# An attention and SwiGLU kernel rewritten: 128-token groups of two batches, quadrant matmuls, DMA transposes, a fixed order

## The chip, the cores and the metric

The kernel runs on one core of one Trainium2 chip. The metric is device time in microseconds (us), read from whole executions; the profiled span is about 2 us shorter (295.9 against 298.2 in the kernel before). In the profile PE is TensorE (PEld its weight loads), DVE is VectorE, ACT is ScalarE, POOL is GpSimd and SP is SyncE. The profile calls the DMAs issued by SP and ACT "hardware" and those issued by POOL "software"; the kernels use the latter where a load also casts. DMA busy shares are means over the core's 16 DMA engines. A DMA "lands" when all its bytes are there; the "tail" is the time from the last matmul to the end of the span; PEclk is the share of TensorE's full clock that was granted. "Crossbar" stands for the DMA transposes, and a "quad" for four small matmuls in the four quadrants of TensorE.

## The reference

Linear attention with decay over blocks feeds a SwiGLU layer. Batch 4, 8 heads, 768 tokens, head size 64; FFN 512 to 1536 to 512. Inputs and output are fp32.

```python
for b in range(nb):                       # blocks of tokens
    intra = (qb @ kb.T) * Dmask           # lam ** (i - j), causal
    out   = intra @ vb + (qb * lam_pow) @ kv_state
    kv_state = lam_block * kv_state + (kb * rev_pow).T @ vb
x = out.transpose(0, 2, 1, 3).reshape(B * S, H * D)     # 3072 x 512
y = (silu(x @ w_gate) * (x @ w_val)) @ w_out
```

Both kernels use blocks of 128 tokens, which gives the same result, and bf16 operands.

## The kernel before

It loads whole sequences by batch and head pair, transposes q and k on TensorE, runs attention batch by batch, and interleaves it with FFN tiles of 512 tokens.

## Time and profile before

Three executions took 298.16 to 298.25 us, median 298.21.

| Reading | Value | View |
|---|---|---|
| span | 295.9 us | page |
| PE busy | 87% | page |
| first FFN matmul | 52.6 us | timeline |
| 864 FFN matmuls at 0.216 us | 187 us | timeline (own product) |
| tail after the last matmul | 3.6 us | timeline |

The page cuts the span in 40 slices of 7.4 us; digits are busy tenths, the last row is what DMA moved.

```profile
PE   0233614999999999999999999999999999999995
PEclk9999999999999999999999999999999999999999
DMA  9999999999999110990001000100100000001012
GB/s 153 169 169 189 209 189 157 172 182 194 168 128 115 37 39 35 73 124 35 2 35 38 34 5 35 39 0 35 38 15 23 35 35 8 29 37 38 35 72 106
```

For seven slices PE is mostly idle (6 tenths at most) and the DMA engines are full (a 9 in every slice). After that PE is in nine tenths of every slice at full clock, and the stores cause only about 35 GB/s.

The table of stretches for the same kernel (start:end, length, busy time and instructions of each engine, granted clock, DMA share, GB/s) shows the same start:

```profile
30.00:40.00 10.00, 4.41 (x54) 2.48 (x54) 4.40 (x11) 1.74 (x7) 0.82 (x1) 1.00 1.10 210
40.00:50.00 10.00, 2.90 (x36) 1.65 (x35) 4.59 (x11) 0.87 (x4) 2.76 (x4) 1.00 1.61 164
50.00:60.00 10.00, 9.81 (x87) 4.19 (x84) 5.12 (x14) 4.64 (x13) 4.94 (x7) 1.00 1.74 170
```

### The profile page before, as it was taken

How to read it: one execution, taken by the hardware profiler on the slowest of the kernel's cores; microseconds unless marked ns; L12 is line 12 of the kernel's file. 1: busy time of each engine (PE TensorE's matmuls, PEld its weight loads, DVE VectorE, ACT ScalarE, POOL GpSimd, SP SyncE). 2: the span in 40 equal slices, each digit the busy share in tenths (PEclk: the TensorE clock that was granted, in tenths of full speed). 3: DMA queues.
4: the chain of work that ended last, by engine and by line, in shares of the span. 5: the costliest groups of instructions: out<-in, count | busy, mean ns of one | idle time of the engine just before them, and what ended most of it. 6: DMA issues, size and time to landing. Idle time of an engine off the chain costs nothing.

```text
span 295.9 us, 4660 instructions
## 1 busy us (share of the span) xinstructions
PE 256.3 (87%) x1824; PEld 119.3 (40%) x1824; DVE 127.2 (43%) x296; ACT 96.6 (33%) x232; POOL 57.0 (19%) x78
## 2 busy tenths in 40 slices
PE   0233614999999999999999999999999999999995
PEld 0122302446444444464444445544444444444442
DVE  1662525477654533934453444345344433222200
ACT  3411201536342422263333224524322332222321
POOL 9765015453156000840000000000000000000000
PEclk9999999999999999999999999999999999999999
DMA  9999999999999110990001000100100000001012
GB/s 153 169 169 189 209 189 157 172 182 194 168 128 115 37 39 35 73 124 35 2 35 38 34 5 35 39 0 35 38 15 23 35 35 8 29 37 38 35 72 106
DMA packets 81383, 23.90 MB, mean 81 GB/s; under 512 B 75729, under 2 KB 77265, under 8 KB 81361
## 3 DMA queue, kind: packets, MB, share of 16 engines
q0 software_dynamic: 52816, 11.02, 41.8%
q1 hardware_dynamic: 28544, 12.59, 19.9%
q8 instruction: 14, 0.23, 0.3%
q14 instruction: 9, 0.07, 0.1%
HBM read 28.32 MB, written 6.29 MB: 117 GB/s over the span
## 4 chain that ended last, share of the span: by engine, by line
PE 82%; DMA 13%; POOL 1%; DVE 1%; issue 1%; ACT 0%; SPq 0%; ACTq 0%; DVEq 0%; POOLq 0%
PE gp L255 24%; PE vp L261 22%; PE ffn_op L272 22%; DMA v_raw<-in_v_dram 8%; PE op L225 3%; DMA q_nat<-in_q_dram 3%; PE sp L196 3%; PE op L217 3%; DMA k_nat<-in_k_dram 2%; PE tpq L171 2%; PE tpk L177 1%; PE up L232 1%; DVE ssb L204 1%; PE sp L198 1%; DVE v_s L163 0%
## 5 line engine op out<-in xcount | busy, mean ns | idle before, releaser
L263 DVE TENSOR_TENSOR h_sb<-sil,vp 128x512 bf16<-128x512 bf16 x72 | 49.5, 687 | 83.7 <-PE vp L261 81.1
L272 PE MATMUL ffn_op<-wo_sb,h_sb 128*128 128x512 bf16 x288 | 65.4, 379 | 0.2
L258 ACT ACTIVATE sil<-gp 128x512 bf16<-128x512 f32 x72 | 43.0, 598 | 60.6 <-PE gp L255 60.2
L204 DVE TENSOR_TENSOR ssb<-sp,maskp_all 128x512 bf16<-128x512 f32 x48 | 33.0, 686 | 32.5 <-PE sp L198 32.5
L261 PEld LDWEIGHTS <-wv_sb 128*128 128x128 bf16 x288 | 28.0, 98 | 35.0 <-issue 3.1
L272 PEld LDWEIGHTS <-h_sb 128*128 128x128 bf16 x288 | 27.7, 98 | 31.9 <-issue 0.2
L99 POOL DMA_DIRECT2D k_nat<-in_k_dram x32 | 26.4, 830 | 52.6 <-PE up L234 24.6
L275 ACT COPY osb<-ffn_op 128x512 f32<-128x512 f32 x24 | 14.1, 586 | 62.7 <-PE ffn_op L272 62.7
L255 PEld LDWEIGHTS <-wg_sb 128*128 128x128 bf16 x288 | 23.5, 98 | 22.9 <-issue 0.3
L98 POOL DMA_DIRECT2D q_nat<-in_q_dram x32 | 26.6, 833 | 18.8 <-DMA wg_sb<-in_moe_w_gate_dram 7.3
L255 PE MATMUL gp<-xT_285,wg_sb 128*128 128x512 bf16 x72 | 28.1, 390 | 0.0
L255 PE MATMUL gp<-xT_286,wg_sb 128*128 128x512 bf16 x72 | 27.6, 383 | 0.0
L255 PE MATMUL gp<-xT_287,wg_sb 128*128 128x512 bf16 x72 | 27.6, 383 | 0.0
L255 PE MATMUL gp<-xT_288,wg_sb 128*128 128x512 bf16 x72 | 27.6, 383 | 0.0
L261 PE MATMUL vp<-xT_285,wv_sb 128*128 128x512 bf16 x72 | 27.5, 382 | 0.0
L261 PE MATMUL vp<-xT_286,wv_sb 128*128 128x512 bf16 x72 | 27.5, 382 | 0.0
L261 PE MATMUL vp<-xT_287,wv_sb 128*128 128x512 bf16 x72 | 27.3, 379 | 0.0
L261 PE MATMUL vp<-xT_288,wv_sb 128*128 128x512 bf16 x72 | 27.3, 379 | 0.0
L171 PE MATMUL tpq<-identity,q_nat 128*128 128x128 bf16 x96 | 9.2, 240 | 20.1 <-DMA q_nat<-in_q_dram 20.1
L225 PE MATMUL op<-ssb,v_s 128*64 128x128 bf16 x96 | 15.0, 241 | 12.4 <-DVE ssb L204 12.4
L178 ACT COPY kT<-tpk 128x768 bf16<-128x768 bf16 x16 | 12.8, 799 | 23.2 <-PE tpk L177 23.0
L198 PE MATMUL sp<-qT,kT 64*128 64x128 bf16 x96 | 16.4, 237 | 0.0
(90 smaller groups left out, 264.2 us busy)
## 6 DMA issues: line engine op xcount, KB each, us to landing
v_raw<-in_v_dram SPq DMA_DIRECT2D x32, 192.0 KB, 9.4
out_dram<-osb SPq DMA_DIRECT2D x24, 256.0 KB, 2.0
q_nat<-in_q_dram POOLq DMA_DIRECT2D x32, 96.0 KB, 9.5
k_nat<-in_k_dram POOLq DMA_DIRECT2D x32, 96.0 KB, 9.7
wg_sb<-in_moe_w_gate_dram POOLq DMA_DIRECT2D x1, 1536.0 KB, 17.1
wv_sb<-in_moe_w_val_dram POOLq DMA_DIRECT2D x1, 1536.0 KB, 24.5
wo_sb<-in_moe_w_out_dram POOLq DMA_DIRECT2D x1, 1536.0 KB, 18.5
lam_bcast<-in_lam_dram POOLq DMA_DIRECT2D x1, 4.0 KB, 4.1
```

The lines of the kernel that those rows point to most:

```text
L98: nc.gpsimd.dma_start(out=q_nat[:, :, h2, :], in_=q_5d[b, hp, h2])
L99: nc.gpsimd.dma_start(out=k_nat[:, :, h2, :], in_=k_5d[b, hp, h2])
L171: nc.tensor.transpose(tpq[:, blk, :], q_nat[:, blk, :, :], identity)
L198: nc.tensor.matmul(sp[:, 1, cs], st["kT"][64:128, bs], st["qT"][64:128, bs], start=True, stop=True)
L204: nc.vector.tensor_tensor(out=ssb, in0=sp_ap, in1=mp_ap, op=ALU.mult)
L225: nc.tensor.matmul(op[0:64, :], st["v_s"][:, blk, 0, :], ssb[:, 0, ci, :], start=False, stop=True)
L255: nc.tensor.matmul(gp, wg_sb[:, mc, fs], xT[mc][:, ts], start=(mc == 0), stop=(mc == MCHUNKS - 1))
L258: nc.scalar.activation(sil, gp, AF.Silu)
L261: nc.tensor.matmul(vp, wv_sb[:, mc, fs], xT[mc][:, ts], start=(mc == 0), stop=(mc == MCHUNKS - 1))
L263: nc.vector.tensor_tensor(out=h_sb[:, fc, :], in0=sil, in1=vp, op=ALU.mult)
L272: nc.tensor.matmul(op, h_sb[:, fc, sub * TSUB:(sub + 1) * TSUB], wo_sb[:, fc, :], start=(fc == 0), stop=(fc == FCHUNKS - 1))
L275: nc.scalar.copy(out=osb, in_=op)
```

## The change

The intent: start the FFN as soon as 128 tokens are there, pack attention into four 64x64 quadrants of TensorE, take q/k transposes off TensorE, and keep a fixed order. A group is one block of two batches; partition `b2*64 + m` holds tokens `2m` and `2m+1`, which makes the rows of v, and those of q and k in groups 0 and 1, 512 bytes. The diff is long; its core, shortened, with comments added and some lines joined:

```diff
+    NG = NBLK * B // 2                      # 12 groups
+    def gsrc(t, g, b2, extra, dims):        # two tokens in each partition
+        return bass.AP(..., ap=[[2 * D, M]] + dims)
+    # groups 0 and 1: fp32 on the hardware queues, then cast; weights in pieces of 128 or 256 columns
+    w_piece(0, 1); w_piece(1, 2); v_scale(1, nc.gpsimd); w_piece(2, 4); ...; load_qk_shd(2); ...
+    # groups 2 to 11: q and k cast by software DMA, 8 issues of 64 partitions a group
+    def prefetch(g):
+        load_qk_shd(g); load_v(g); dma_transpose(g)      # groups 4 to 11
+    def dma_transpose(g):
+        nc.sync.dma_start(out=..., in_=..., transpose=True)   # 128 x 2048 bf16
+    # scores, intra and state update: 32 matmuls each in quadrants
+    for s in range(2):
+        for b2 in range(2):
+            for h2 in range(2):
+                nc.tensor.matmul(sp[(c, h2)][b2 * M:b2 * M + M, n:n + BLK],
+                                 tt[dp, 0, s, hp, b2 * M:b2 * M + M],
+                                 tt[dp, 1, :, hp, b2 * M:b2 * M + M], ...)
...
-            nc.sync.dma_start(out=out[t0:t0 + TSUB, :], in_=osb)
+            eng.dma_start(out=bass.AP(tensor=out.tensor, offset=out.offset + row * DM + c0,
+                                      ap=[[DM, 2], [2 * DM, M], [1, c1 - c0]]),
+                          in_=osb[:, c0:c1])
...
+    # fixed order, t = block, fc = FFN column of 12
+    at(3, attend, 2 * t + 2, False); at(8, attend, 2 * t + 3, False)
+    at(2, v_scale, 2 * t + 2, nc.gpsimd); at(6, v_scale, 2 * t + 3, nc.gpsimd)
+    at(4, prefetch, 2 * t + 4); at(9, prefetch, 2 * t + 5)
```

The tokens inside a block now stand in the order even, odd. The store puts them back with a three-dimensional pattern: 2 parities, 64 rows, columns.

## The prediction

> **What bounds the kernel now.** The page shows PE busy 87% of a 295.9 us span; PE stands in nine tenths of every slice from about 52 us to the end, at full granted clock. The timeline shows a 512-column FFN matmul starting every 0.216 us; 864 of them are 187 us, a floor that the change keeps. From the matmul starts between 50 and 250 us I work out 45 us for attention (0.056 us per transpose, 0.075 us per pair of 128-column halves, about 0.1 us more at each change of shape). The first 52 us are loading: the table of stretches gives 0 to 4.4 us of PE per 10 us there while DMA moves 156 to 210 GB/s, and the chain of waits is v_raw, q_nat and k_nat landings. So 296 = 52 (start, with 4 blocks of attention) + 187 FFN + 45 attention + about 9 stalls + 4 tail.
>
> **What the change does.**
> 1. Start. Only 128 tokens of two batches must land (1.5 MB in 512-byte rows on two hardware queues), not whole sequences, and weights come in pieces in the order of use. At the old start's rate, q/k/v of groups 0 and 1 (3 MB) are in by about 16 us. I expect the first FFN matmul at about 19 us instead of 52: 33 us less, minus about 8 us of attention that the old start had hidden.
> 2. Attention on PE. 128 of 192 transposes go to the DMA crossbar (7 us less). Scores, intra and state updates become 64x64 quadrants: 96 small matmuls a group in 24 quads. A quad costs between 0.075 us (all four overlap) and 0.146 us (two old pairs in series). [...]so I take the middle; no trace yet shows it. With 8 state matmuls of 0.056 us and four shape changes, 2.7 to 4.4 us a group, about 38 us for eleven groups after the start.
> 3. DMA transposes, new: 8 of 512 KB.[...]
> 4. q/k still come as 128-byte packets (0.032 us each), eight issues of about 0.8 us on POOL per group. POOL also takes v scaling and state copies, and issues stand in order behind them. Loads of group 6 and later start only after state copies of two groups before, 13 us before use against 16 us of PE work: small stalls. Group 4's loads wait behind all weights; I expect 8 us of stall where the first FFN block ends, and a few us in it from late weights.
>
> **Sum.** 19 + 187 + 38 + 12 stalls + 3 tail = 259 span; the fixed order was probably tuned, so I put the time (2.3 us over the span) at 256 us, range 244 to 272. Faster by over 2%: 0.96; within: 0.02; slower: 0.02.
>
> **What would show it.** First FFN matmul at 17 to 22 us; FFN spacing 0.216 us; attention 3 to 4 us of PE per group; PE gaps named after qkt (DMA transpose) and weights of the first block, ending at 55 to 65 us; later blocks under 3 us of gaps each.
>
> **What would make it wrong.** DMA transposes of 10 us or more (stall in each block, over 280); quads that serialize fully or are limited by issue (over 270); POOL scaling v slowly and delaying loads; or all prefetches in time (under 245).

The sum came to a span of 259 us, put at a time of 256 us. The 38 us is the middle of the range for a group, about 3.5 us, times eleven, and no term was named for the DMA transposes.

## More of the kernel before

What the argument touches:

```python
# loads: per batch and head pair, whole sequences; q and k are cast on the way
nc.gpsimd.dma_start(out=q_nat[:, :, h2, :], in_=q_5d[b, hp, h2])
nc.gpsimd.dma_start(out=k_nat[:, :, h2, :], in_=k_5d[b, hp, h2])
nc.sync.dma_start(out=v_raw[:, :, h2, :], in_=v_5d[b, hp, h2])
...
# weights: three whole loads, behind the first batch
nc.gpsimd.dma_start(out=wg_sb, in_=moe_w_gate.rearrange("(c p) f -> p c f", p=128))
...
# output: one store of 128 rows, outer dimension 128
nc.scalar.copy(out=osb, in_=op)
nc.sync.dma_start(out=out[t0:t0 + TSUB, :], in_=osb)
```

The page's list of DMA issues (what, queue, count, size, median us from issue to landing) has the store:

```profile
out_dram<-osb SPq DMA_DIRECT2D x24, 256.0 KB, 2.0
```

## The result

The changed kernel is correct and slower: 330.39 us median of four runs (329.47 to 331.26) against 298.19 us. The ratio is 1.1078, interval 1.1049 to 1.1106. Here and below a ratio is the mean time of one kernel's fast runs over that of the other's of the same rounds, so it is not quite the ratio of the medians.

The page of the changed kernel, slices of 8.2 us:

```profile
PE   7546996734999209999407999806999999999700
PEclk9695799585999858999955999955999999999965
DMA  7999999999309199119399117499310101011111
GB/s 131 199 200 206 160 135 174 114 107 177 72 31 82 46 152 166 37 34 62 53 122 195 30 34 64 57 111 114 75 37 22 47 22 37 27 48 31 51 51 39
```

There are four holes in the PE row, each with a 5 (half of the full clock) in the PEclk row at its end or right behind it, and two empty slices at the end.

The waits (engine, line of the kernel, waited for: us in total, times, longest):

```profile
PE bank L266 <- DMA qkt<-qk: 51.1, 4, 14.9
PE bank L297 <- POOL v_s L181: 4.7, 1, 4.7
```

L266 is the scores. They wait for the DMA transpose four times, up to 15 us each; L297, the intra matmuls, waited once for scaled v in the first block. What that transpose itself waited for shows in the chain that ended last (start, us, what), around the hole at 109 to 123 us:

```profile
97.50 3.54 POOL qk L191 x6
...
102.18 14.06 DMA qk<-in_q_dram
...
116.49 6.98 DMA qkt<-qk
123.47 0.04 issue
123.51 1.07 PE bank L266 x32
124.58 1.82 PE bank L352 x4
```

The transpose took 7 us. Before it, the last of eight 64 KB loads of q and k took 14 us from issue to landing. The table of stretches says that the DMA engines were far from full at that time:

```profile
101.00:113.00 12.00, 7.80 (x103) 4.08 (x100) 4.01 (x7) 2.36 (x4) 6.35 (x10) 0.99 0.58 64
```

They moved 64 GB/s at a share of 0.58 while a load needed 14 us. At the start (10 to 30 us) they moved 200 at a share of 1.2 to 1.4 (the share adds up the times of all packets and can exceed 1).

The timeline of the end (start, us, engine, line, what) shows the other place:

```profile
299.75 10.52 PE L369 MATMUL bank<-wo_sb,h 128*128 128x512 bf16 x48
310.71 3.55 ACTq L377 DMA_DIRECT2D out_dram<-osb  x1
310.71 0.42 DVE L376 COPY osb<-bank 128x256 f32<-128x256 f32 x1 [9.93 <-ACT osb L376]
311.17 0.66 SPq L377 DMA_DIRECT2D out_dram<-osb  x1
```

The last matmul ends at 310.3 us and the last instruction is at 311, but the span ends at 328.7: 18.5 us are stores that haven't landed.

The packet records explain both. Each of these kernels stores 128 packets of 2 KB per output tile. The table gives, for stores with nothing beside them, the time from the first packet's start to the last one's end, the mean time of a packet, and packets in flight (worked out as 128 times the mean packet over the duration):

| Kernel | shape of the store | one store alone | mean packet | in flight |
|---|---|---|---|---|
| before | 128 x 512 | 0.82 us | 86 ns | 13 |
| changed | 2 x 64 x 512 | 6.24 us | 101 ns | 2.1 |

A store of the changed kernel has about two packets in flight (2.1), not thirteen. The slowest dimension of its pattern is 2, that of the store before 128. Two kernels that differ in much else don't show that this dimension sets the packets in flight; e5 and e6 below test it.

The packet records also show what this does to the loads. From 150 to 153 us, with no store under way, 560 to 900 packets of q and k started per us. From 157 to 165 us, beside two stores in turn, it was 17 to 29 per us, about one for each store packet (18 to 20 per us), while the table of stretches has the engines nearly idle (share 0.16, 44 GB/s):

```profile
157.00:165.00 8.00, 2.88 (x80) 1.84 (x78) 3.32 (x6) 0.60 (x2) 3.40 (x7) 0.93 0.16 44
```

So most of the loads' packets had passed (3896 of this group's 4096 had started by 157 us), and the rest came about one for one with the store's. In e1 below, 380 to 900 packets of q and k started per us beside the split store.

So the question for experiments: does this one line cause the long waits, or do the DMA transposes, which stand in the waits by name?

What went as intended: FFN matmuls still start every 0.216 us at full clock, and attention became cheaper than predicted. One group on TensorE, from the timeline:

```profile
107.34 0.61 PE L287 MATMUL bank<-qkt,kvz 128*128 128x128 bf16 x8
107.88 0.64 PE L297 MATMUL bank<-ssb,v_s 64*64 64x128 bf16 x32
108.35 0.45 PE L321 MATMUL bank<-v_s,qk 64*64 64x64 bf16 x32
123.51 1.07 PE L266 MATMUL bank<-qkt 64*64 64x128 bf16 x32 [14.71 <-DMA qkt<-qk]
```

By the starts after 60 us, a group costs about 2.2 us (0.8 scores on average, 0.6 to 0.7 at full clock and 1.0 at half; 0.5 state times q, 0.5 intra, 0.3 to 0.45 state update). Four quadrants do overlap: the median distance of two starts is 4 to 5 ns.

### The profile page after: what moved, and what is told of

Read it like the earlier page. It is cut to its first block, busy times and chain, and to the rows that moved or that the text cites. A ratio compares the mean times of both kernels' runs of the same rounds, so it can differ in the third digit from the quotient of the medians.

```text
span 328.7 us, 5235 instructions
## 1 busy us (share of the span) xinstructions
PE 238.8 (73%) x2164; PEld 119.1 (36%) x2164; DVE 105.4 (32%) x185; ACT 72.0 (22%) x122; POOL 120.6 (37%) x185
## 4 chain that ended last, share of the span: by engine, by line
PE 42%; DMA 34%; POOL 13%; DVE 2%; issue 2%; ACT 0%; ACTq 0%; SPq 0%; DVEq 0%; POOLq 0%
PE bank L369 14%; PE bank L352 13%; DMA qk<-in_q_dram 12%; PE bank L359 12%; DMA qkt<-qk 10%; DMA v<-in_v_dram 6%; POOL qk L191 6%; DMA wv_sb<-in_moe_w_val_dram 5%; POOL kvz L335 2%; POOL v_s L181 2%; PE bank L266 2%; POOL kvl L337 1%; POOL wg_sb L171 1%; PE bank L297 1%; DVE xt L310 1%
## 5 line engine op out<-in xcount | busy, mean ns | idle before, releaser
L362 DVE TENSOR_TENSOR h<-sil,bank 128x512 bf16<-128x512 bf16 (+1 forms) x74 | 49.7, 672 | 124.8 <-ACT sil L356 68.3
L352 PE MATMUL bank<-xt,wg_sb 128*128 128x512 bf16 (+1 forms) x296 | 81.5, 402 | 4.8 <-DMA wg_sb<-in_moe_w_gate_dram 4.0
L359 PE MATMUL bank<-xt,wv_sb 128*128 128x512 bf16 (+1 forms) x296 | 78.6, 391 | 1.6 <-DMA wv_sb<-in_moe_w_val_dram 1.6
L356 ACT ACTIVATE sil<-bank 128x512 bf16<-128x512 f32 (+1 forms) x74 | 43.3, 586 | 153.0 <-PE bank L352 145.8
L369 PE MATMUL bank<-wo_sb,h 128*128 128x512 bf16 x288 | 65.6, 379 | 0.0
L273 DVE TENSOR_TENSOR ssb<-bank,mask 128x512 bf16<-128x512 f32 x52 | 33.9, 683 | 49.1 <-PE bank L266 49.1
L266 PE MATMUL bank<-qkt 64*64 64x128 bf16 x416 | 10.9, 260 | 52.9 <-DMA qkt<-qk 51.1
L369 PEld LDWEIGHTS <-h 128*128 128x128 bf16 x288 | 28.2, 98 | 34.0
L181 POOL TENSOR_TENSOR v_s<-v,rev 128x1024 bf16<-128x1024 f32 x12 | 23.2, 1933 | 16.7 <-DMA v<-in_v_dram 16.6
L191 POOL DMA_DIRECT2D qk<-in_q_dram x40 | 27.8, 744 | 3.1 <-DMA wv_sb<-in_moe_w_val_dram 1.7
L191 POOL DMA_DIRECT2D qk<-in_k_dram x40 | 27.7, 718 | 2.9 <-DMA wv_sb<-in_moe_w_val_dram 1.6
L266 PEld LDWEIGHTS <-qkt 64*64 64x64 bf16 x416 | 8.6, 133 | 54.4 <-DMA qkt<-qk 51.6
L297 PE MATMUL bank<-ssb,v_s 64*64 64x128 bf16 x384 | 8.8, 234 | 5.4 <-POOL v_s L181 4.7
L297 PEld LDWEIGHTS <-v_s 64*64 64x64 bf16 x384 | 6.5, 116 | 7.7 <-POOL v_s L181 4.9
```

The costliest lines, as they stand in the source:

```text
L181: eng.tensor_tensor(out=st[("vs", g)][:, h0:h1], in0=st[("v", g)][:, h0:h1].rearrange("p h (s d) -> p h s d", s=2), in1=bap(rev, [[2, h1 - ...
L191: nc.gpsimd.dma_start(out=t[b2 * M:b2 * M + M, i, s].rearrange("p (h d) -> p h d", h=H), in_=gsrc(src, g, b2, s * D, [[S * D, H], [1, D]]))
L266: nc.tensor.matmul(sp[(c, h2)][b2 * M:b2 * M + M, n:n + BLK], tt[dp, 0, s, hp, b2 * M:b2 * M + M], tt[dp, 1, :, hp, b2 * M:b2 * M + M], st ...
L273: nc.vector.tensor_tensor(out=ssb[:, h2, 2 * c:2 * c + 2].rearrange("p a s n -> p (a s n)"), in0=sp[(c, h2)], in1=mask[:, h2, 2 * c:2 * c ...
L297: nc.tensor.matmul(op[b2][h2 * 64:h2 * 64 + 64, hp * BLK:hp * BLK + BLK], v_s[ps, 2 * hp + h2, s], ssb[ps, h2, hp, s], start=(blk == 0 and ...
L352: nc.tensor.matmul(gp[:, 0:N], wg_sb[:, mc, fs], xt[:, mc, b0:b1].rearrange("p b n -> p (b n)"), start=(mc == 0), stop=(mc == MC - 1))
```

## The experiments

Theory A: the stores, with two packets in flight, hold up the q/k loads beside them and queue at the end. By an estimate one store then takes 5.6 us: 128 packets of 88 ns, the mean of the last four stores of the changed kernel, two at a time; with four at a time it is 2.8 us. Theory B: the DMA transposes, and where they stand in the order, cost the time; the store is innocent. Each kernel was timed in turn with the kernel before on the same chip, so kernels are best compared by ratio.

The author spoke of A in numbers of DMA engines ("2eng" and "store16" in the labels come from that). No packet record names an engine, so these passages are cut from the expectations, along with A's reasoning in e1 and e4 that rested on them; their ranges stand.

| Run | Median us (range) | Ratio to before | Result |
|---|---|---|---|
| changed | 330.4 (329.5 to 331.3) | 1.108 | correct |
| e1_store16 | 275.6 (275.2 to 277.5) | 0.926 | correct |
| e2_pe_transpose | 308.8 (306.6 to 311.4) | 1.033 | correct |
| e3_early_loads | 290.4 (290.3 to 290.7) | 0.974 | correct |
| e4_before_2eng | 315.3 (314.6 to 316.0) | 1.057 | wrong on purpose |
| e5_store64x2 | 272.4 (271.2 to 274.1) | 0.913 | wrong on purpose |
| e6_store4x32 | 302.3 (301.2 to 306.5) | 1.011 | wrong on purpose |
| e7_store16_early | 269.3 (268.4 to 270.0) | 0.902 | correct |
| b1_all | 264.9 (264.1 to 265.6) | 0.886 | correct |
| e8_store16_pe | 273.0 (272.0 to 273.8; one of 614.9 left out) | 0.915 | correct |
| e8b_store16_pe (again) | 271.4 (270.5 to 272.7) | 0.910 | correct |
| b2_natural_rows | 265.1 (264.4 to 265.7) | 0.889 | correct |
| b3_vscale_first | 258.4 (254.5 to 259.3) | 0.858 | correct |

Medians are over all runs of a row unless it says otherwise, ratios over fast runs alone (for b3 the three of 254.5 to 257.8 us).

### e1_store16: the store in two halves of 64 rows

```diff
-            eng.dma_start(out=bass.AP(..., offset=out.offset + row * DM + c0,
-                                      ap=[[DM, 2], [2 * DM, M], [1, c1 - c0]]),
-                          in_=osb[:, c0:c1])
+            for s in range(2):
+                eng.dma_start(out=bass.AP(..., offset=out.offset + (row + s) * DM + c0,
+                                          ap=[[2 * DM, M], [1, c1 - c0]]),
+                              in_=osb[s * M:s * M + M, c0:c1])
```

> Changed kernel with each output store cut into two 64-row stores, one per token parity, so that the slowest dimension of each is 64 and not 2. Theory A[...]: a store lands in under 3 us, q/k loads of groups 6, 8 and 10 land about 3 to 7 us after their last issue instead of 14, the four long waits of the scores for the DMA transpose shrink from about 15 us to 4 to 7 us for three of them, the tail after the last matmul falls from 18 us to under 5 us; total 275 to 295 us. Theory B (the DMA transposes themselves and their place in the order are the cause, the store is innocent): only the tail moves if anything, waits stay at 12 us or more, total 312 to 330 us.

It took 275.6 us, 55 us less than the changed kernel. The tail is 4.8 us, and the waits for the transpose fell:

```profile
PE bank L266 <- DMA qkt<-qk: 14.2, 4, 8.1
```

The chain at the former hole, with the transpose in its place and 4.4 us long, and no load in it:

```profile
104.21 0.21 PE bank L352
104.42 4.38 DMA qkt<-qk
108.80 0.04 issue
108.85 0.64 PE bank L266 x32
```

The last q load of groups 6, 8 and 10 landed 3.6, 3.7 and 3.9 us after its issue, against 14.1, 14.1 and 9.5 in the changed kernel. Three waits are now 1.6 to 2.3 us, shorter than the 4 to 7 expected. Theory B's 312 us is refuted.

### e2_pe_transpose: no DMA transposes, the store as it was

```diff
-            dma_transpose(g)
+    # pe_transpose(g) one FFN column before the scores, attend(..., True)
```

> Changed kernel with all groups transposed on TensorE (as groups 0 to 3 are already) instead of 8 groups by DMA transpose; the stores are left as they are. Theory A[...]: each long wait loses only the 7 to 10 us of the DMA transpose and keeps the late landing; tail stays 18 us; total 300 to 318 us. Theory B (DMA transposes are the cause): waits vanish, total under 295 us.

It took 308.8 us, inside the range of A and outside that of B. The scores' place in the list of waits is taken by the transposes on TensorE:

```profile
PE bank L227 <- DMA qk<-in_q_dram: 17.3, 5, 8.0
```

The holes stay (8.0 us at 104, 6.7 us at 153), now before the TensorE transposes and for the q load; the tail is still 18.5 us. The DMA transpose was 7 to 10 us of each chain, and taking it out gave 22 us in all.

### e3_early_loads: loads earlier, the store as it was

```diff
-                at(4, prefetch, 2 * t + 4)
-                at(9, prefetch, 2 * t + 5)
+                at(0, prefetch, 2 * t + 4)
+                at(4, prefetch, 2 * t + 5)
```

> Changed kernel with the loads (and DMA transpose) of each group issued 4 to 5 FFN columns earlier from the second block on, before the state copies in the GpSimd queue; stores left as they are. Theory A: [...]have about 13 us more time, so the long waits from the second block on shrink from 15 to about 2 to 8 us; the tail stays 18 us; total 295 to 315 us. If the waits do not shrink at all, the place of the loads in the order is not part of the cause.

It took 290.4 us, better than expected. The q loads still take 11 to 15 us to land in the middle blocks, but only one later wait is left (5.4 us). The slow loads hurt only because they were issued late; either cure removes the waits, and only the store cures the tail (18.4 us here).

### e4_before_2eng: the store's form alone, in the kernel before

```diff
-            nc.sync.dma_start(out=out[t0:t0 + TSUB, :], in_=osb)
+            nc.sync.dma_start(out=bass.AP(..., ap=[[DM, 2], [2 * DM, 64], [1, DM]]), in_=osb)
```

> Kernel before, with its output stores written in the changed kernel's three-dimensional form (slowest dimension 2); rows of each 128 come out permuted, so the result is wrong on purpose. Theory A: [...]the four last stores queue and the tail grows by 10 to 15 us, total 306 to 316 us, with the middle of the kernel little changed. If the store's form does not matter, 298 us.

It took 315.3 us: 17 us more from this line alone. Each store lasts 6.2 us, the tail is 19.9 us instead of 3.6 (16 us more, where 10 to 15 were expected), and the middle is unchanged. PE stands in nine tenths until the last matmul. It costs less here probably because most loads are over before the first stores begin at 98 us, and nothing waits closely for the rest.

### e5_store64x2 and e6_store4x32: is it the slowest dimension?

```diff
-   ap=[[DM, 2], [2 * DM, M], [1, c1 - c0]]
+   ap=[[2 * DM, M], [DM, 2], [1, c1 - c0]]      # e5: 64 outermost
+   ap=[[DM, 4], [4 * DM, 32], [1, c1 - c0]]     # e6: 4 outermost
```

> Changed kernel, each output store still one DMA of three dimensions, but with the order of its first two dimensions turned (64 by 2 instead of 2 by 64), so that the slowest is 64; the rows come out permuted, the result is wrong on purpose. If the size of the slowest dimension decides [...]the kernel takes the 273 to 279 us of the split store. If it was the splitting into two DMAs that helped, it stays at 325 to 331 us.

> Changed kernel, one store of three dimensions with a slowest dimension of 4 (rows permuted, wrong on purpose). [...]a store lasts about 2.8 us instead of 5.6; the q/k loads are held up about half as long, the tail is 6 to 9 us, and the total lies between: 285 to 305 us.

| Slowest dimension | one store alone | in flight | tail us | last q load of group 6, landing | median us |
|---|---|---|---|---|---|
| 2 (changed) | 6.24 us | 2.1 | 18.5 | 14.1 us | 330.4 |
| 4 (e6) | 4.3 us | 3.7 | 10.4 | 10.4 us | 302.3 |
| 64 (e5) | 0.82 us | 13 | 3.9 | 3.1 us | 272.4 |

e5 has one DMA per store, the same bytes and the same number of dimensions, and only the order of two dimensions differs; it keeps all of e1's gain and 3 us more, just under its range. So splitting wasn't what helped. Nor was it the order of the rows in memory: e5 writes them one after another, e1 every second one, as the changed kernel does, and both are fast. The waits of e5:

```profile
PE bank L266 <- DMA qkt<-qk: 13.9, 4, 10.0
```

e6 lies between, as expected, but a store took 4.3 us, not 2.8, because a packet took 126 ns there and not 86 to 101 (why isn't known), and the tail is 10.4 us, not 6 to 9. Its profile is from a run slow by its time (306 us), so its tail is only indicative.

### e7_store16_early: both cures

The edits of e1 and e3 together.

> Split stores and early loads together. The remaining waits of the scores from the second block on (1.6 to 2.3 us each in the run with split stores alone[...]) go; the wait before group 4 (8 us) and the late first block stay. Theory: 266 to 271 us. If the early loads gave all their gain by dodging the stores only, 273 to 276 us.

It took 269.3 us, in the range. No wait over 0.7 us is left after the first block. What remains is the first block: PE idle for 4.3 us at 56 and for 7.9 us at 70.

### e8_store16_pe: is the crossbar worth it?

The edits of e1 and e2 together.

> Split stores, and all groups transposed on TensorE (no DMA transpose at all), loads where the changed kernel has them. Against the split stores alone (275.6 us): if the DMA transpose is now the longest piece of what the scores wait for, the waits before groups 4, 6, 8 and 10 (8.1, 1.6, 2.2, 2.3 us) go, but 128 transposes (0.9 us a group on TensorE, 7 us in all) come back: 270 to 277 us. Clearly faster than 268 us would say that the DMA transposes cost more than those waits show; over 280 us that the crossbar earns its place.

> The same kernel as the run with split stores and all transposes on TensorE, again, because its profiled execution was an outlier of 615 us beside three of 272 to 274 us: 271 to 275 us, and a profile in which the waits before groups 6, 8 and 10 are under 1 us and q/k transposes on TensorE take about 0.9 us a group.

The first submission took 272.0 to 273.8 us in three runs and 614.9 us in the profiled one. There FFN matmuls started every 0.621 us throughout and no change of the clock was recorded. What did this isn't known; it isn't used. The repetition gave 271.4 us. Without the crossbar the waits for q and k are gone (0.4 us at most), and the total is about 4 us better than e1: in this order DMA transposes gained nothing, since 128 transposes on TensorE (0.9 us a group, 7 us in all) cost less than the waits for eight DMAs (14.2 us in e1).

### b1_all, b2_natural_rows, b3_vscale_first: a better version

b1 has e7 and a new order of POOL's queue at the start. v of groups 2 and 3 was issued at once on a hardware queue, beside the first weights; it now stands behind them. v scaling of group 1 stood in front of the weights in POOL's queue, waiting 4 us for its data, and went to DVE with those of groups 2 and 3.

```diff
     w_piece(1, 2)
-    v_scale(1, nc.gpsimd)
     w_piece(2, 4)
...
-    load_v(2)
-    load_v(3)
+    load_fp32(2, nc.gpsimd, v, "v", b2)         # in the queue, after the weights in use first
...
+            at(2, prefetch, 4); at(2, wo_piece, 0, 6); at(2, wo_piece, 6, 12); at(2, prefetch, 5)
```

> Split stores, early loads, and a new order of the GpSimd queue at the start: v of groups 2 and 3 comes behind the first weights in the same queue, v scaling of groups 1 to 3 is on VectorE, loads of groups 4 and 5 stand before and after the w_out pieces instead of behind v scaling. The first block should end at 55 to 62 us instead of 76; total 250 to 262 us. If the first block is bound by the rate of the DMA engines and not by order, it ends after 68 us and the total stays above 264 us.

It took 264.9 us, missing its range. The first block ended at 74.3 us (scores of group 4), so time and end both fell where the expectation's other theory, the rate of the DMA engines, had put them. b3 below gains 6 us more by order, so the rate alone isn't the limit. The wait for group 4 grew from 7.9 to 11.3 us: its DMA transpose now ran beside the w_out load (seen in the trace, not tested alone).

b2 writes the tokens back in order with the attention output, so the store is one plain DMA of 128 rows, and transposes group 4 on TensorE:

```diff
-                o = xt[:, :, 2 * bp + b2]
+                o = xt[:, :, 2 * bp + b2].rearrange("p h (m s) -> p h s m", s=2)
-    (store in two halves)
+            eng.dma_start(out=out[row:row + BLK, c0:c1], in_=osb[:, c0:c1])
-            dma_transpose(g)
+            if g > 4:
+                dma_transpose(g)
```

> All changes of the version with the new start (264.9 us), and two more: the tokens are put back in their natural order when the attention output is written, so that a store is one DMA of 128 rows (0.82 us in the kernel before instead of 1.41 us for two halves), and group 4 alone is transposed on TensorE, because its DMA transpose runs beside the w_out load and holds the scores for 11.3 us. The wait before scores of group 4 should fall under 3 us, the rest stays: 253 to 258 us. If the wait only moves to another load of that time, 259 to 264 us.

It took 265.1 us, no gain, and 1 us over even the range for a wait that only moves: it moved. Waits of b2:

```profile
PE bank L297 <- POOL v_s L181: 8.6, 1, 8.6
```

The scaled v of group 4 was now late, because in POOL's queue it stood behind state copies and the load issues of group 6. b3 puts the scaling first, and for groups 4 and 5 on DVE; it also loads w_out in four pieces instead of two (not shown):

```diff
-                at(2, v_scale, 2 * t + 2, nc.gpsimd)
-                at(6, v_scale, 2 * t + 3, nc.gpsimd)
+                at(0, v_scale, 2 * t + 2, nc.vector if t == 1 else nc.gpsimd)
+                at(4, v_scale, 2 * t + 3, nc.vector if t == 1 else nc.gpsimd)
                 at(0, prefetch, 2 * t + 4)
```

> The previous best with the next order mended: v scaling of each group stands before the loads of the next groups, for groups 4 and 5 on VectorE, and w_out comes in four pieces. The 8.6 us wait of the output matmuls of group 4 for its scaled v should go: 254 to 259 us. If the wait only moves to another transfer once more, 261 to 265 us, and the first 90 us are then bound by what the DMA engines move, not by this order.

It took 258.4 us (0.858 of the kernel before, by its fast runs), in its range, correct and the best. The runs spread more (254.5 to 259.3), and three of six count as over 1.5% above its fastest. Its page, slices of 6.4 us:

```profile
PE   8283789956897999999999999999999999999994
PEclk9657569997999999999999999999999999999999
```

From the fourteenth slice on PE is in nine tenths of every slice but the last. The first FFN matmul is still at 26.4 us.

## Why the prediction was wrong

The prediction said 256 us (244 to 272) and faster; it was 330.4 us and slower. Its sum against the changed kernel's trace:

| Term | predicted us | measured us |
|---|---|---|
| first FFN matmul | 19 | 25.1 |
| 864 FFN matmuls at full clock | 187 | 187 |
| attention on PE after that | 38 | 27 |
| stalls (PE idle, gaps over 0.7 us, after the first FFN matmuls) | 12 | 57 |
| matmuls at half clock after them | none | 8 |
| tail | 3 | 18.5 |
| rest (short gaps) | none | 6 |

- **Right:** the FFN spacing, the attention by quadrants, and the direction of the start (25 instead of 52 us). Quads were even better than the range: 2.2 us a group, not 2.7 to 4.4.
- **The step that failed** is in the sum, "12 stalls + 3 tail", and under it step 4: "13 us before use against 16 us of PE work: small stalls". The store was not costed at all. The new pattern stood in the diff and was read as the old store. It has 2.1 packets in flight instead of 13, lasts 6.2 us instead of 0.82, and makes the loads beside it land 14 us after issue instead of 4. For group 6 the loads were first issued 11.4 us before PE was ready for its scores, near the predicted 13, but from there to the end of the transpose took 26.1 us; in e1 it took 13.0 us. Turning the pattern round (e1, e5) takes off 55 to 58 us, three quarters of the distance to the predicted time and more than all of the loss against before. Tail and waits are shown separately: in e4 the tail grows by 16 us while the middle stays, and in e1 the three later waits fall from 11.8 to 14.9 us to 1.6 to 2.3 us.
- **DMA transposes** have no term of their own in the sum, and the figure for the time of one rested on no trace. The chains show 7 to 10 us in the changed kernel and 4.4 to 7.8 us in e1; from its issue on SP to its last packet one takes 3.8 to 5.6 us even there. The wait that the prediction named after qkt was therefore a real one, but e2 shows that it was worth 22 us here, and e8b that it costs about 4 us once the stores are right.
- **The first block** was put at 55 to 65 us for its end; scores of group 4 start at 78.8. The 8 us stall named there was real (9.7 us), but came on top of a late scaled v (4.7 us, behind load issues and state copies in POOL's queue) and a late first weight (first FFN matmul at 25.1 us): hardware loads of v went beside the weights, and a waiting v scaling stood ahead of the third piece. b3 shows that order matters in this block, but for the first weight that cause isn't shown: b1 brought the first FFN matmul to 23.3 us, b2 and b3 have it at 26.0 and 26.4. There two more v loads stand on SP beside the weights, because group 4's DMA transpose, behind which they waited in b1, is gone; this fits the cause but wasn't tested alone. With three waits in turn taking each other's place, it is hard to see which comes next.
- **Half clock.** Not in the prediction. In this trace the granted clock was 0.5 after each hole of 4.7 us or more, and FFN matmuls started every 0.43 us. 36 of them cost about 36 x 0.21 = 8 us. In e1 a shorter wait, of 2.2 us, was followed by 3.4 us at half clock, those of 1.6 and 2.3 us were not; what sets the difference isn't shown. This is a cost of the waits and not a cause of its own.

What stays open: the packet records name no engine. Shown are the packets in flight (2.1, 3.7 and 13 for a slowest dimension of 2, 4 and 64), not what makes them so. Why the late packets of q and k wait isn't shown either, only that they came about one for one with the store's (17 to 29 beside 18 to 20 per us), and that the last q load of group 6 landed after 14.1 us while such stores were under way and after 3.6 us in e1, without them.

## What to carry to other kernels

Look at the first dimension of every DMA pattern that a layout change touches: here a pattern that starts with a 2 ran with 2.1 packets in flight, and the loads beside it landed after 14.1 us instead of 3.6, although it moved few bytes (256 KB a store). When a transfer lands late while the DMA share and the GB/s are low (here 0.58 and 64), look for such a DMA beside it and not only at the name that the wait carries. Undo the layout where it is cheap (here in the copy that writes the operand: 0.73 us instead of 0.59 on ACT and 0.69 on DVE), so that the store is plain again, and issue loads early enough that one slow landing doesn't matter.
